# Windowed attention and a gated feed-forward on one core: a first batch ordered by hand, masks added by TensorE, V loaded in place, and y placed behind its a and b

## The chip, the cores and the metric

The kernel runs on one core of a Trainium2 chip. The metric is the device time of one execution in microseconds, as the median of several runs. A profile of one execution was taken by the hardware profiler; its span, the time from the first to the last instruction, was 281.5 us where that run took 283.2 us. The engines are TensorE (matrix products, written to PSUM, a memory of eight banks), VectorE, ScalarE, GpSimd (here used to start the loads) and SyncE (here used to start the stores). Each engine takes its instructions strictly in the order of its own queue, and the engines wait for one another on semaphores.

## The reference

Two parts follow each other. The first is attention over q, k, v of 8 batches, 8 heads, 576 positions and 64 channels. A query sees only keys behind it: in heads 0 to 3 the last 32 positions ("plain"), in heads 4 to 7 the last 32 positions of every fourth ("dilated").

```python
scores = scale * np.matmul(q, k.transpose(0, 1, 3, 2))
rel = pos[:, None] - pos[None, :]
mask_plain = (rel >= 0) & (rel < window)                                  # window = 32
mask_dil = (rel >= 0) & (rel < window * dilation) & (rel % dilation == 0) # dilation = 4
masks = [mask_plain if h < H // 2 else mask_dil for h in range(H)]
attn = softmax(np.where(masks, scores, -1e9))
x = (attn @ v).transpose(0, 2, 1, 3).reshape(B * S, H * D)   # 4608 tokens x 512
a = x @ w1                                                   # 512 -> 1024
b = x @ w2
out = ((a * b) @ w3) @ w_out                                 # 1024 -> 1024 -> 512
```

## The kernel before

**Loads.** All inputs are f32 in HBM and are cast to bf16 by the transfers, which GpSimd starts. `load_qk` fetches q and k of a batch, `load_vp` the values of the plain heads in overlapping blocks of 128 keys, `load_vd` those of the dilated heads into a staging tile `vst`, from which `spread_vd` (L147) copies them to `vd`, where each block of 64 values stands beside a column of ones. The ones make the value product give the softmax's sum as a 65th column. `load_w12`, `load_wo` and `load_w3` fetch the weights. The first loads are, in order: q and k of batch 0's dilated heads, the constants of GpSimd, `vst`, q and k of the plain heads, `vp`, the first halves of w1 and w2, all of batch 1, the second halves of w1 and w2, w_out, and w3 in four pieces.

**Attention.** A batch is four steps: dilated heads, first and second half of the positions (called d0 and d1), then plain heads, first and second half (p0 and p1). u is 1 for the dilated heads and 0 for the plain ones. Before them VectorE transposes q and k, so that channels lie on partitions (`transpose_qk`, L222 and L229). A step has three phases:

- `scores` (L258): for four heads and three blocks of 96 queries, products with the 128 keys of the block, in two halves of 32 channels, so that the four heads use the four quarters of the rows of the array. All go to `ps_a`, four PSUM banks. ScalarE takes exp of all four heads (L269) into `et`, and VectorE multiplies `et` by a mask of ones and zeros (L272). In batch 0 exp and mask work on two heads at a time.
- `values` (L297): 12 products of `et` with the values into the rest of the same banks (in batch 0 into two banks of their own, `ps_e`), then VectorE takes the reciprocal of the sums (L305) and multiplies (L306) into `xo`.
- `to_channels` (L323): six transposes on TensorE into the bank `ps_x`, and a copy into `XT`, the transposed x that lasts for the whole kernel (L338 on ScalarE for the dilated heads, L336 on VectorE for the plain ones).

**Feed-forward.** Tokens go in 9 tiles of 512. `ffn1(t, f)` makes, for one of 8 blocks f of 128 hidden channels, a and then b, of four matmuls of 512 columns each (L425), both into banks `f` of a ring of three. ScalarE copies a to `asb` (L435); VectorE multiplies b by it into `gt` (L436). Since nothing stands between w3 and w_out, the kernel makes their product once: `fuse_t` transposes a block of w3 on TensorE into `ps_x` (L474) and ScalarE copies it to `w3T` (L480); `fuse_m` multiplies it by w_out (L488) and VectorE copies it to `wf_sb` (L495). `ffn2(t, tb)` makes y for 128 tokens with eight matmuls (L458), ScalarE copies it to `osb` (L466, three buffers) and SyncE stores it.

**Order.** The kernel writes every engine's order by hand. Batch 0 runs first, alone. Then comes the first tile's a and b, the fusing, the second tile's a and b, the first tile's y, and from then on the a and b of tile t interleaved with the y of tile t-1: two f, then one block of y. The attention phases of the batches from 1 on are put between the groups of matmuls: `point()` is called before each a, each b and each half of a y or of a fused product, counts the calls and runs as many phases as the table `marks` asks for at that count. `later` appends a phase to the list, `behind` attaches work to the last one. Phases of the steady part come every second point, ahead of an a or of a y. Work attached with `behind`, such as the transposes of the next q and k, follows the values phase on VectorE.

The softmax here doesn't subtract the row's maximum and nothing guards it: scores larger than these inputs give would overflow.

## Time and profile before

| | |
|---|---|
| median of 3 runs | 283.26 us (283.12 to 283.83) |
| span of the profile | 281.5 us |
| TensorE busy | 245.9 us (87%) |
| VectorE busy | 160.1 us (57%) |
| ScalarE busy | 117.8 us (42%) |
| first matmul of a tile (L425) starts | 25.94 us |
| first transposes of w3 (L474) start | 44.41 us |
| a and b of the second tile start | 71.27 us |
| a and b of the third tile start | 105.01 us |
| L425 | 550 matmuls recorded, mean 387 ns |
| L458 | 282 matmuls recorded, mean 379 ns |

The starts are read from TensorE's timeline. A matmul's duration in these lists includes the time that it spends in the pipeline behind its forerunner, so the distance between starts, not the duration, says how fast a stream runs. A releaser in brackets, such as `[3.49 <-DVE kt L222]`, says how long the engine sat idle before the line and which instruction ended the wait. In the names, PE is TensorE, PEld its weight loads, DVE VectorE, ACT ScalarE, POOL GpSimd and SP SyncE.

### The profile page before, as it was taken

The numbers are of one execution on the slowest core, as the hardware profiler recorded it, in microseconds if no ns is written. First come the engines' busy times: TensorE is split into PE (matmuls) and PEld (weight loads), VectorE is DVE, ScalarE is ACT, GpSimd is POOL, SyncE is SP. The second block draws the span as 40 slices with busy tenths as digits, with TensorE's granted clock in tenths as the row PEclk, the third lists the DMA queues.
The fourth block names the chain that finished last, engine by engine and source line by source line (L and its number), as shares of the span: only waits on it lengthen the run. The fifth ranks groups of instructions, "written<-read, shape, count | busy, mean of one in ns | idle before, by whom it ended". The sixth has DMA issues, their size and how long they took to land.

```text
span 281.5 us, 5593 instructions
## 1 busy us (share of the span) xinstructions
PE 245.9 (87%) x2300; PEld 125.7 (45%) x2336; DVE 160.1 (57%) x328; ACT 117.8 (42%) x172; POOL 53.6 (19%) x77
## 2 busy tenths in 40 slices
PE   0355987788958899999999999999999999999994
PEld 0243434454424444545554545545545544444441
DVE  5662268455796776776777777766744632122210
ACT  1552235552435345535433554454345332432331
POOL 8943512450070060024006000000000000000000
PEclk9999999999989999999999999999999999999998
DMA  7999999999179289589747912110111121111233
GB/s 104 155 204 194 194 210 211 208 186 178 9 131 148 30 157 225 90 131 156 109 88 126 172 42 60 55 41 37 40 37 40 37 75 40 48 64 40 57 82 123
DMA packets 50745, 30.50 MB, mean 108 GB/s; under 512 B 37920, under 2 KB 40992, under 8 KB 50720
## 3 DMA queue, kind: packets, MB, share of 16 engines
q0 software_dynamic: 45088, 20.71, 58.7%
q1 hardware_dynamic: 5632, 9.44, 10.8%
q8 instruction: 18, 0.29, 0.4%
q14 instruction: 7, 0.06, 0.1%
HBM read 41.41 MB, written 9.44 MB: 181 GB/s over the span
## 4 chain that ended last, share of the span: by engine, by line
PE 75%; DMA 9%; DVE 6%; POOL 3%; ACT 3%; issue 2%; POOLq 0%; ACTq 0%; DVEq 0%
PE f L425 39%; PE f L458 22%; DMA qn<-in_q_dram 5%; DMA w_sb<-in_moe_w_dram 4%; PE ps_a L258 4%; PE f L488 4%; PE ps_a L297 3%; PE ps_x L323 3%; DVE xo L306 2%; ACT w3T L480 1%; PE ps_x L474 1%; POOL vst L136 1%; DVE gt L436 1%; DVE qt L229 1%; ACT et L269 1%
## 5 line engine op out<-in xcount | busy, mean ns | idle before, releaser
L425 PE MATMUL f<-XT,w_sb 128*128 128x512 bf16 x550 | 136.5, 387 | 3.4 <-issue 0.9
L436 DVE TENSOR_TENSOR gt<-f,asb 128x512 bf16<-128x512 f32 x72 | 49.6, 689 | 63.8 <-PE f L425 61.5
L425 PEld LDWEIGHTS <-w_sb 128*128 128x128 bf16 x576 | 53.6, 99 | 62.6 <-issue 5.8
L458 PE MATMUL f<-wf_sb,gt 128*128 128x512 bf16 x282 | 67.2, 379 | 0.4 <-issue 0.2
L435 ACT CAST asb<-f 128x512 bf16<-128x512 f32 x72 | 42.3, 587 | 53.4 <-PE f L425 52.0
L466 ACT COPY osb<-f 128x512 f32<-128x512 f32 x36 | 21.1, 586 | 70.2 <-PE f L458 68.2
L269 ACT ACTIVATE et<-ps_a 128x1152 bf16<-128x1152 f32 (+1 forms) x36 | 36.5, 1026 | 18.3 <-PE ps_a L258 18.3
L458 PEld LDWEIGHTS <-gt 128*128 128x128 bf16 x288 | 26.5, 98 | 28.5
L258 PE MATMUL ps_a<-qt,kt 32*128 32x96 bf16 x768 | 15.1, 211 | 18.5 <-DVE kt L229 7.9
L306 DVE TENSOR_TENSOR xo<-ps_a,rcp 96x768 bf16<-96x768 f32 x28 | 26.7, 953 | 1.0
L258 PEld LDWEIGHTS <-kt 32*128 32x128 bf16 x768 | 10.9, 97 | 30.5 <-issue 16.9
L136 POOL DMA_DIRECT2D vst<-in_v_dram x32 | 21.2, 669 | 14.1 <-DMA w3n<-in_moe_w_dram 4.4
L229 DVE STREAM_TRANSPOSE qt<-qn 128x160 uint32<-128x160 uint32 (+1 forms) x64 | 19.6, 420 | 2.3 <-DMA qn<-in_q_dram 2.3
L272 DVE TENSOR_TENSOR et<-et,mask_pl 128x1152 bf16<-128x1152 bf16 (+1 forms) x18 | 12.4, 692 | 14.3 <-ACT et L269 14.2
L297 PEld LDWEIGHTS <-et 128*128 128x128 bf16 x384 | 16.9, 102 | 7.4 <-issue 1.4
L323 PE MATMUL ps_x<-ident,xo 96*128 96x96 bf16 x192 | 14.4, 214 | 6.6 <-DVE xo L306 4.0
L323 PEld LDWEIGHTS <-xo 96*128 96x128 bf16 x192 | 12.0, 102 | 14.3 <-DVE xo L306 5.2
L272 DVE TENSOR_TENSOR et<-et,mask_di 128x1152 bf16<-128x1152 bf16 (+1 forms) x18 | 12.3, 687 | 9.8 <-ACT et L269 9.7
L112 POOL DMA_DIRECT2D qn<-in_q_dram x9 | 6.2, 690 | 57.8 <-DVE qt L229 54.6
L488 PE MATMUL f<-wo_sb,w3T 128*128 128x512 bf16 x60 | 15.1, 379 | 0.4 <-issue 0.3
L338 ACT COPY XT<-ps_x 128x576 bf16<-128x576 bf16 x18 | 11.5, 640 | 9.2 <-PE ps_x L323 9.1
L480 ACT COPY w3T<-ps_x 128x1024 bf16<-128x1024 bf16 x8 | 8.1, 1012 | 8.4 <-PE ps_x L474 8.4
(45 smaller groups left out, 111.3 us busy)
## 6 DMA issues: line engine op xcount, KB each, us to landing
qn<-in_q_dram POOLq DMA_DIRECT2D x7, 576.0 KB, 6.1
kn<-in_k_dram POOLq DMA_DIRECT2D x7, 576.0 KB, 7.8
vp<-in_v_dram POOLq DMA_DIRECT2D x7, 384.0 KB, 10.5
w_sb<-in_moe_w_dram POOLq DMA_DIRECT2D x4, 512.0 KB, 11.5
w3n<-in_moe_w_dram POOLq DMA_DIRECT2D x4, 512.0 KB, 18.7
out_dram<-osb SPq DMA_DIRECT2D x8, 256.0 KB, 2.3
out_dram<-osb SPq DMA_DIRECT2D x8, 224.0 KB, 2.4
out_dram<-osb SPq DMA_DIRECT2D x8, 192.0 KB, 2.2
```

The costliest lines, as they stand in the source:

```text
L136: nc.gpsimd.dma_start(out=vsts[b % 2][p0 : p0 + n, m, :, :], in_=bass.AP(tensor=x.tensor, offset=x.offset + (4 * i0 + 2 * second) * D, ap= ...
L258: nc.tensor.matmul(out=ps_a[:, h, c0 : c0 + 96], lhsT=kt[prt, 96 * m : 96 * m + P, c], rhs=rhs, start=(c == 0), stop=(c == 1),)
L269: nc.scalar.activation(out=ev, in_=ps_a[:, h : h + n, 0:HALF], func=ACT.Exp, scale=scale)
L272: nc.vector.tensor_tensor(out=ev, in0=ev, in1=mk.unsqueeze(1).to_broadcast([P, n, HALF]), op=AL.mult)
L297: nc.tensor.matmul(out=ov[:, j // ns, j % ns, :], lhsT=self.et[:, c0 : c0 + P], rhs=rhs, start=True, stop=True,)
L306: nc.vector.tensor_tensor(out=xo[0:96].rearrange("p h j d -> p (h j) d").rearrange("p (n s) d -> p n s d", n=nb), in0=ov[0:96, :, :, 0:D], ...
L323: nc.tensor.transpose(out=xo, in_=self.xo[0:96, hp, 2 * m : 2 * m + 2, :], identity=ident[0:96, 0:96],)
L425: nc.tensor.matmul(out=ps, lhsT=w_sb[:, c, f * P : (f + 1) * P], rhs=XT[:, c, t0 + lo : t0 + hi], start=(c == 0), stop=(c == DCH - 1),)
L435: nc.scalar.copy(out=a_sb[:, 0 : hi - lo], in_=ps)
L436: nc.vector.tensor_tensor(out=gts[t][:, f, lo:hi], in0=pss[1], in1=a_sb[:, 0 : hi - lo], op=AL.mult)
L458: nc.tensor.matmul(out=y, lhsT=gts[t][:, f, tb * P : (tb + 1) * P], rhs=wf_sb[:, f, :], start=(f == 0), stop=(f == KFF - 1),)
L488: nc.tensor.matmul(out=ps, lhsT=w3T[ft][:, g, :], rhs=wo_sb[:, g, :], start=(g == 0), stop=(g == KFF - 1),)
```

## The change

The change rewrites the beginning and one thing in the steady part.

- **The first batch is written out by hand** (`first_batch`), in pairs of heads. `scores_of_pair` first lets TensorE put the mask into PSUM, as the product of the identity with a tile of 0 and -30000 (`neg_pl`, `neg_di`), one matmul of 288 columns for each head, and adds the scores to it. So exp gives zeros outside the window, and the multiplication on VectorE goes. The masks of ones and zeros that the later batches use are made at the end of the batch (`const_masks`).
- **PSUM has a layout of its own in that stage**: two pairs of banks for scores (`ps_s`), a ring of three banks for values (`ps_o`), and `ps_x`. Afterwards the seven become the ring `f` of three and `ps_a` of four.
- **V of the dilated heads is loaded straight into place.** A row of `vd` now holds a one, 64 values, 64 values and a one, so that each half position has a one beside it. The staging tile and `spread_vd` go. In `normalize` the sums are the first column for d0 and the last for the others.
- **Loads have another order**: q and k of the plain heads come ahead of V; w1 and w2 come whole, in three pieces each, then w_out in halves, then w3 mixed with batch 1. The plain values of the first three batches are loaded in two transfers. Prefetching of a batch sits one phase later.
- **Batch 1 has a table of points** (`second_batch`): its phases run at points 19 to 38, that is, in the fusing and in the first y.
- **The fused product**: transposes of w3 go to banks of the ring instead of `ps_x`, half of the copies to `w3T` (three buffers now) go to VectorE, and a product is made in two halves with a point ahead of each.
- **y stands right behind its own a and b**: a tile is 8 f, then 4 blocks of y. The first y comes before the second tile's a and b. `osb` has six buffers. The marks are moved, and the phases of the steady part now fall ahead of a b or of the second half of a y.

The core of the diff:

```diff
-    ps_a = psum.tile([P, 4, TB], F32, name="ps_a")
     ps_x = psum.tile([P, 2 * TB], BF16, name="ps_x")
-    ps_e = ps_early.tile([P, 2, TB], F32, name="ps_e")
+    ps_s = [ps_early.tile([P, 2, TB], F32, name=f"ps_s{i}") for i in range(2)]
...
-                out=vsts[b % 2][p0 : p0 + n, m, :, :],
+                out=vds[b % 2][p0 : p0 + n, 4 * m : 4 * m + 4, 16 : 16 + 2 * D],
...
+        def scores_of_pair(self, hp):
+            ps = ps_s[hp]
+            neg = (neg_di if self.u else neg_pl[:, self.hf]).rearrange("p m x -> p (m x)")
+            for g in range(2):
+                nc.tensor.matmul(
+                    out=ps[:, g, 0:HALF], lhsT=ident, rhs=neg, start=True, stop=False
+                )
+            self.score_matmuls((2 * hp, 2 * hp + 1), lambda h: ps[:, h % 2], False)
+            nc.scalar.activation(
+                out=self.probs(2 * hp, 2), in_=ps[:, :, 0:HALF], func=ACT.Exp, scale=scale
+            )
...
+    def first_batch():
+        d0, d1, p0, p1 = steps[0:4]
+        transpose_qk(0, 1, 0)
+        transpose_qk(0, 1, 1)
+        d0.scores_of_pair(0)
+        d0.scores_of_pair(1)
+        transpose_qk(0, 0, 0)
+        transpose_qk(0, 0, 1)
+        d1.scores_of_pair(0)
+        d1.scores_of_pair(1)
+        p0.scores_of_pair(0)
+        p0.scores_of_pair(1)
+        d0.values_of_pair(0)
+        d0.values_of_pair(1)
+        p1.scores_of_pair(0)
+        d1.values_of_pair(0)
+        p1.scores_of_pair(1)
+        d1.values_of_pair(1)
+        d0.to_channels()
+        p0.values_of_pair(0)
+        p0.values_of_pair(1)
+        d1.to_channels()
+        p1.values_of_pair(0)
+        p1.values_of_pair(1)
+        p0.to_channels()
+        p1.to_channels()
+        const_masks()
+        prefetch(2)
...
+            (19, transpose_qk, 1, 1, 0),
+            (20, transpose_qk, 1, 1, 1),
+            (22, d0.scores),
+            (24, d1.scores),
+            (26, d0.values),
+            (28, transpose_qk, 1, 0, 0),
+            (28, d0.to_channels),
+            (28, d1.values),
+            (29, transpose_qk, 1, 0, 1),
+            (30, p0.scores),
+            (30, d1.to_channels),
+            (32, p1.scores),
+            (34, p0.values),
+            (36, p0.to_channels),
+            (36, p1.values),
+            (36, prefetch, 3),
+            (38, p1.to_channels),
...
-        xv = ps_x.rearrange("p (g x) -> p g x", g=KFF)
+        xv = bank().bitcast(BF16).rearrange("p (g x) -> p g x", g=KFF)
...
-        w3T[ft] = wk_pool.tile([P, KFF, P], BF16, tag="w3T", bufs=2, name="w3T")
-        nc.scalar.copy(out=w3T[ft], in_=xv)
+        w3T[ft] = wk_pool.tile([P, KFF, P], BF16, tag="w3T", bufs=3, name="w3T")
+        (nc.vector.tensor_copy if ft % 2 else nc.scalar.copy)(out=w3T[ft], in_=xv)
...
-    load_qk(0, split=True)
+    load_qk(0, 1)
+    const_pool()
+    load_qk(0, 0)
+    load_vd(0)
     load_vp(0)
-    load_w12(0, 512)
-    load_qk(1)
-    load_vd(1)
-    load_vp(1)
-    load_w12(512, 1024)
-    load_wo()
-    for g in range(4):
-        load_w3(g)
+    load_w12(0, 256)
+    load_w12(256, 512)
+    load_w12(512, 1024)
+    load_wo(0)
+    load_wo(1)
+    load_w3(0)
+    load_w3(1)
+    load_qk(1, 1)
+    load_w3(2)
+    load_vd(1)
+    load_w3(3)
+    load_qk(1, 0)
+    load_vp(1)
...
-    for t in range(2, NT):
-        for i in range(4):
-            ffn1(t, 2 * i, point)
-            ffn1(t, 2 * i + 1, point)
-            ffn2(t - 1, i, point)
-    for tb in range(4):
-        ffn2(NT - 1, tb, point)
+    for t in range(1, NT):
+        for f in range(KFF):
+            ffn1(t, f, point)
+        for tb in range(4):
+            ffn2(t, tb, point)
```

## The prediction

> **What bounds the kernel now.** I read the busy times first (TensorE 87% of the span), then the chain of waits, then busy time by stage, with the stage borders taken from TensorE's timeline. The columns are stretch, length, and busy us of TensorE, its weight loads, VectorE, ScalarE and GpSimd.
>
> ```profile
> 7.93:25.94 18.01, 8.05 (x169) 6.76 (x170) 10.41 (x22) 8.59 (x13) 10.55 (x14) 1.00 1.36 191
> 25.94:44.41 18.47, 17.08 (x110) 7.15 (x112) 8.96 (x21) 6.74 (x10) 6.45 (x9) 1.00 1.43 199
> 44.41:71.50 27.09, 21.62 (x247) 13.09 (x251) 14.28 (x24) 11.64 (x12) 8.23 (x10) 1.00 1.43 189
> 71.50:105.46 33.96, 28.49 (x345) 14.55 (x350) 27.30 (x59) 14.88 (x21) 10.50 (x14) 0.95 0.72 96
> 105.46:130.60 25.14, 24.93 (x261) 12.72 (x265) 18.18 (x36) 12.05 (x19) 5.91 (x8) 1.00 0.98 150
> ```
>
> The last line is one tile beside one batch, 25.14 us with TensorE never idle. In the chain it is a repeated pattern of 16 `L425` and 8 `L458` matmuls in 6.285 us. Without attention, from 229 us on, the same 24 take 5.18 us: 0.2158 us a matmul, and 1.10 us of TensorE for one attention step (scores, values, transposes). So the whole program needs, after the first batch, 928 matmuls (9 tiles of 96, 64 for W3·W_out) x 0.2158 = 200.3, 64 weight transposes x 0.058 = 3.7, and 28 steps x 1.1 = 30.8: 234.8 us. Tiles start at 25.94, the last matmul ends at 278.1, and 3.4 us of eviction and store follow. 278.1 - 25.94 - 234.8 = 17.4 us are lost, all before 105.5: some 4 in the second line, 6 in the third and 8 in the fourth. What can be won is there and in the first 25.94 us.
>
> ```profile
> 5.52 1.20 DVE L229 STREAM_TRANSPOSE qt<-qn 128x160 uint32<-128x160 uint32 x4 [1.15 <-DMA qn<-in_q_dram]
> ...
> 11.49 1.22 DVE L229 STREAM_TRANSPOSE qt<-qn 128x160 uint32<-128x160 uint32 x4 [1.16 <-DMA qn<-in_q_dram]
> ...
> 14.39 1.24 DVE L222 STREAM_TRANSPOSE kt<-kn 128x576 uint32<-128x576 uint32 x1
> ...
> 15.69 0.67 PE L258 MATMUL ps_a<-qt,kt 32*128 32x96 bf16 x24 [3.49 <-DVE kt L222]
> ...
> 24.55 0.66 PE L323 MATMUL ps_x<-ident,xo 96*128 96x96 bf16 x6 [1.31 <-DVE xo L306]
> ...
> 25.25 0.64 ACT L338 COPY XT<-ps_x 128x576 bf16<-128x576 bf16 x1 [1.99 <-PE ps_x L323]
> 25.94 0.58 PE L425 MATMUL f<-XT,w_sb 128*128 128x512 bf16 x1 [0.73 <-ACT XT L338]
> ```
>
> In the first batch the plain heads' q is transposed only at 11.49 and their k at 14.39, though VectorE could have done so at 8.1. Every step's scores, mask, values, normalising and transposing follow one another. The last XT copy ends at 25.89 and tiles start.
>
> ```profile
> 19.14 1.43 POOL L129 DMA_DIRECT2D vp<-in_v_dram  x1 [1.83 <-DMA w_sb<-in_moe_w_dram]
> ...
> 52.40 0.70 POOL L112 DMA_DIRECT2D qn<-in_q_dram  x1 [1.27 <-DMA w3n<-in_moe_w_dram]
> ```
>
> GpSimd waits in the brackets are landings: its eight DMA semaphores go round, so an issue waits for the one eight before it. The first w1 half landed at 19.1 and all of w3 at 52.4. In destination bytes the loads up to there are 2,396 KB and 8,892 KB: 195 KB/us.
>
> ```profile
> 123.50 0.44 PE L258 MATMUL ps_a<-qt,kt 32*128 32x96 bf16 x24
> ...
> 124.08 1.14 ACT L269 ACTIVATE et<-ps_a 128x1152 bf16<-128x1152 f32 x1
> ...
> 125.11 0.59 ACT L435 CAST asb<-f 128x512 bf16<-128x512 f32 x1
> 125.25 0.76 DVE L272 TENSOR_TENSOR et<-et,mask_di 128x1152 bf16<-128x1152 bf16 x1 [0.69 <-ACT et L269]
> ...
> 125.93 0.68 DVE L436 TENSOR_TENSOR gt<-f,asb 128x512 bf16<-128x512 f32 x1
> ...
> 127.59 0.53 PE L297 MATMUL ps_a<-vd,et 128*128 128x65 bf16 x12
> ...
> 128.47 0.22 DVE L305 RECIPROCAL rcp<-ps_a 96x12 f32<-96x12 f32 x1
> 128.73 0.95 DVE L306 TENSOR_TENSOR xo<-ps_a,rcp 96x768 bf16<-96x768 f32 x1
> 129.60 1.24 DVE L229 STREAM_TRANSPOSE qt<-qn 128x160 uint32<-128x160 uint32 x4
> ...
> 129.78 0.44 PE L258 MATMUL ps_a<-qt,kt 32*128 32x96 bf16 x24
> ```
>
> This is the steady step. Scores at 123.50 give `et` at 125.22 and the mask at 125.25 to 125.93. VectorE takes work in order, so `gt`, whose b was filled by then, starts only at 125.93. Values at 127.59 occupy VectorE from 128.47 to 129.60 and a transpose of 1.1 us follows; the next scores at 129.78 come just after `xo`.
>
> **What the Trainium skill says.** "TensorE: Matmul & The Clock Gate", What's actually happening: the array runs at 1.2 GHz until it was busy for about 3.4 us, then at 2.4. The trace agrees: the first ten `L425` matmuls, from 26.7, are 0.427 us apart, later ones 0.216. The same page, Back-to-back issue gap: N/1.2 ns cold, N/2.4 + 2.5 warm; that prices a 288-column mask matmul at 0.24 or 0.12 us, which no run here shows yet. "TensorEngine Tiling (Array Packing)", Key Properties: row tiles work in parallel, and changing the mode drains the array. By the price above 24 scores of 96 columns would take 1.9 us cold one after another; they take 0.67, so four heads do run together, and with two heads I expect half the rate. "VectorE: DVE Perf Modes", The perf-mode tier table: copies from PSUM reach at most 2x. The 128x576 XT copy takes 0.45 us on VectorE, so 1024 bf16 elements take about 0.7 us (estimate), against 1.01 on ScalarE.
>
> **The change part by part.**
>
> *First batch.* Removed: 8 mask multiplications (0.45 us each), the 1.47 us spread of V on ScalarE, and the late q and k loads (now issued at about 4.2 instead of 6.83). Added: 16 mask matmuls, 3.8 us cold, and scores at half the rate, 8 pairs x 0.48 cold. Chain: k transposed at 8.0, first exp at 8.65 as now. q and k of the plain heads land at 8.5 to 10 and are transposed by 11.5. Eight exps of 0.65 us on two score buffers come every 0.75 to 1.0 us, the last two after `et` 0 is free at about 13.8: all by 16. Eight normalisings are 0.2 + 0.5 us (half of 0.95), so 6 us of VectorE, from 13.6, when vd lands; vp lands at about 16.5, as now. They end at 20.2 to 21.3. Then a transpose (0.45) and XT (0.64) give the tile start: 21.3 warm, 23.2 cold. I take 22.0, with the array warm from the dense score work, so the first tile does not pay its ten cold matmuls (2.1 us).
>
> *Load order.* w1 and w2 come before batch 1, in pieces. At 200 KB/us from vp on: first pieces at 19.2, last at 26.8, wanted at 29; w_out 31.8; w3 from 34.3, wanted at 36; batch 1's dilated q, k 38.2 and 39.7, plain 48.3 and 49.7. All are hidden by the tile's own matmuls.
>
> *First tile.* No attention is inside it now: 22.0 + 13.8 + 0.2 = 36.0 (now 44.41).
>
> *Fusing W3·W_out with batch 1, then the first y.* Half the w3T copies go to VectorE and w3 transposes get banks from the ring of three instead of ps_x, which takes away the waits of both kinds of transpose on one bank. I followed the built order against the durations above. VectorE then carries 8 wf_sb copies (0.62 pitch), 4 w3T (0.7), 4 transposes (1.1), 4 masks (0.7), 4 normalisings (1.2), 2 XT copies (0.45): 20.7 us. Its queue is solid from about 48 to 56, and the plain k transpose comes at 54.7 to 55.95. The plain scores, ordered ahead of the second half of the seventh product, stand in TensorE's queue from 53.45 to 56.05 and hold everything behind them: 2.6 us. In all 3.2 us lost. Needed: 17.5 + 6.9 + 4.4 = 28.8, so the second tile starts at 68.0. The kernel now has done the same work at about 78 (71.3 plus the 6.9 us of the first y).
>
> *Second tile.* The transposes of batch 2 run on VectorE beside the end of the first y. Then `gt` stands behind a transpose or a mask that waits for exp; three banks give b only some 2.0 us until its bank is wanted (a, transposes and b of the next). By the built order about 1.0 us is lost at the second b and 0.9 at three of the scores behind `xo`, smaller bits elsewhere: 4.7 of 30.5. Third tile from 98.5.
>
> *Tiles 3 to 7, y right behind.* Nothing is saved on TensorE, which has no gaps there. The b's come every 1.73 us for 13.8 us, and the attention pieces now fall between a and b instead of ahead of a. After scores, exp waits for a's copy on ScalarE and `gt` for the mask, and ends 3.4 us after the scores' start; its bank is wanted after b, a, transposes and b, at 3.2: 0.2 to 0.25 us late. After values, `gt` waits for normalising and a transpose: again about 0.25. Three or four such places are 0.8 us a tile, 4.0 in five tiles. y's last matmul of the first group needs the last `gt` 0.9 us after b; seven matmuls (1.5 us) cover that. Six osb buffers, V in place (0.55 us less VectorE a batch), prefetch one phase later: hidden, or in the above.
>
> *Sum.* 22.0 + 234.8 + 3.4 + lost 0.2 + 3.2 + 4.7 + 4.0 = 272.3 span. The profiled span is 1.8 below the time (281.5 against 283.26): **274.0 us**.
>
> **The rivals.**
> A: grouping costs nothing and the first batch is warm early. Tile start 21.3, lost 0.2 + 3.2 + 3.0 (second tile): 265.9 span, 267.7 us. For it: ScalarE and VectorE have average room in a tile (12 and 18 of 25 us). Against it: order on VectorE, not its sum, makes the waits.
> B: the middle stages lose what they lose now, 6.3 and 7.8 us in place of 3.2 and 4.7: 6.2 more, 280.2 us. For it: VectorE is 80% busy from 71.5 to 105.5, and nothing of that load but the spread goes. Against it: the weight transposes' waits on ps_x go.
> C: the ring of three banks becomes the bound. The only stretch of now that has a's and b's without y's between, 71.3 to 95.4, holds 13.8 us of matmuls and 4.1 of attention, and lost 6.2. Half of that for each of five tiles, since attention is thinner there, is 15.5 instead of 4.0: 285.5 us, slower than before. Against it: per tile VectorE has 6 us of room.
>
> **How the numbers follow.** The forecast has 0.50, A 0.25, B 0.17, C 0.08. A, B and the forecast are faster; C is slower, and a time within 0.3% is left 0.01 of that: 0.92 faster, 0.01 same, 0.07 slower. The range takes in A's end less a little and B's plus a little, 267 to 281. The ends of the unknown costs (mask matmuls cold or warm: 1.9 us at the start and up to 2.1 in the first tile; bank waits 0 to 1.5 us a tile) lie within it.
>
> **What would show it.** Right: the first tile's matmuls start at 21 to 23.5, at 0.216 apart; the second tile's at 66 to 71; a wait of TensorE for the plain k transpose in the fusing stage; idle TensorE of 0.3 to 1.5 us in each of tiles 3 to 7, ended by `gt`. Wrong: a first matmul after 24.5; waits for w_sb or w3n above 1 us; 27 us or more for a tile beside attention; gapless tiles of 25.1 would make A right.

## The result and the profile after

The changed kernel takes 271.99 us (median of 4 runs, 269.81 to 273.12), beside 283.19 us for the kernel before on the same chip: a ratio of 0.9605, 95% interval 0.9531 to 0.9679. The profiled run has a span of 270.2 us (281.5 before). Forecast were 274.0 us and a span of 272.3, so the total was near. Some terms of the sum were not, and the total is near in part by luck: errors in both directions cancelled, as worked out below. All ratios leave out executions in a slower state, of which the experiments had one (with the old order of the loads).

| start of | before | forecast | after |
|---|---|---|---|
| first tile | 25.94 | 22.0 | 23.50 |
| fusing | 44.41 | 36.0 | 39.09 |
| second tile, same work done | 78.2 | 68.0 | 70.54 |
| third tile, same work done | 111.9 | 98.5 | 100.05 |
| end of the span | 281.5 | 272.3 | 270.2 |

(For before, 6.9 us, the first y, are added to 71.27 and to 105.01, since the changed kernel has then done one y more.) The lead over before grows from 2.4 us to 5.3, 7.7 and 11.9, and stays (11.3 at the end): the gain is made ahead of 100 us. Busy time by stage, cut at those starts (stretch, length, busy us of TensorE, its weight loads, VectorE, ScalarE and GpSimd with instructions in brackets, granted clock, DMA share, GB/s):

```profile
7.80:23.50 15.70, 14.11 (x183) 9.26 (x183) 8.70 (x24) 7.75 (x12) 10.46 (x14) 1.00 1.53 184
23.50:39.09 15.59, 15.59 (x64) 6.70 (x64) 4.84 (x7) 4.68 (x8) 4.63 (x7) 1.00 1.17 210
39.09:70.54 31.45, 28.95 (x329) 16.23 (x328) 22.60 (x48) 11.49 (x13) 14.24 (x18) 1.00 1.54 196
70.54:100.05 29.51, 26.99 (x325) 13.71 (x324) 22.27 (x46) 14.76 (x20) 6.91 (x9) 1.00 0.91 137
100.05:125.20 25.15, 25.15 (x265) 12.72 (x264) 18.10 (x36) 12.23 (x18) 5.50 (x7) 1.00 0.86 121
```

In the first line TensorE is busy 14.11 of 15.70 us, where before it was busy for 8.05 of 18.01: most of the first batch is now bound by TensorE. In the second it never idles, but the same 64 matmuls take 15.59 us instead of the 13.8 that they need. In the third 2.5 us are idle and in the fourth as many. The last is a tile beside attention with y right behind, as the next ones are: TensorE is busy the whole of it, and it takes what such a tile took before (25.15, the next 25.14).

The first batch in the timeline (start, duration, engine, line, operation):

```profile
8.39 0.66 PE L280 MATMUL ps_s<-neg_di,ident 128*128 128x288 bf16 x2
8.49 0.65 ACT L284 ACTIVATE et<-ps_s 128x576 bf16<-128x576 f32 x1 [6.47 <-PE ps_s L264]
...
8.98 0.66 PE L264 MATMUL ps_s<-qt,kt 32*128 32x96 bf16 x12
...
9.57 0.66 PE L280 MATMUL ps_s<-neg_di,ident 128*128 128x288 bf16 x2
9.68 0.65 ACT L284 ACTIVATE et<-ps_s 128x576 bf16<-128x576 f32 x1 [0.54 <-PE ps_s L264]
...
10.87 0.65 ACT L284 ACTIVATE et<-ps_s 128x576 bf16<-128x576 f32 x1 [0.54 <-PE ps_s L264]
...
22.13 0.64 PE L355 MATMUL ps_x<-ident,xo 96*128 96x96 bf16 x6 [0.73 <-ACT XT L370]
...
22.81 0.64 ACT L370 COPY XT<-ps_x 128x576 bf16<-128x576 bf16 x1 [0.73 <-PE ps_x L355]
23.50 6.69 PE L502 MATMUL f<-XT,w_sb 128*128 128x512 bf16 x22 [0.73 <-ACT XT L370]
```

One pair of heads takes 1.19 us of TensorE: from 8.39 to 8.98 two mask matmuls, then 12 scores until 9.57. The exps come at the same distance (8.49, 9.68, 10.87), each after idling for TensorE. At the end, from 18.7 us on, the one bank `ps_x` sets the pace: transposes, 0.64 us of copy, the next transposes, 1.37 us a round. And with all this the array is still slow at 23.50. Its weight loads in the first tile show it:

```profile
25.59 0.15 PEld L502 LDWEIGHTS <-w_sb 128*128 128x128 bf16 x1 [0.27 <-issue]
26.01 0.15 PEld L502 LDWEIGHTS <-w_sb 128*128 128x128 bf16 x1 [0.28 <-issue]
```

0.43 us lie between them, not 0.216, and so on until about 27.2.

The steady step, to be laid beside the one of before:

```profile
101.01 0.45 PE L264 MATMUL ps_a<-qt,kt 32*128 32x96 bf16 x24
...
101.65 1.14 ACT L294 ACTIVATE et<-ps_a 128x1152 bf16<-128x1152 f32 x1
102.82 0.76 DVE L295 TENSOR_TENSOR et<-et,mask_pl 128x1152 bf16<-128x1152 bf16 x1 [1.05 <-ACT et L294]
...
103.39 1.89 PE L502 MATMUL f<-XT,w_sb 128*128 128x512 bf16 x8
103.50 0.68 DVE L513 TENSOR_TENSOR gt<-f,asb 128x512 bf16<-128x512 f32 x1
...
105.11 0.53 PE L306 MATMUL ps_a<-vd,et 128*128 128x65 bf16 x12
...
107.68 1.90 PE L502 MATMUL f<-XT,w_sb 128*128 128x512 bf16 x8
107.89 0.67 DVE L513 TENSOR_TENSOR gt<-f,asb 128x512 bf16<-128x512 f32 x1
```

`gt` still stands behind the mask (102.82, 0.76 us) on VectorE, as before, and is as late again behind normalising and transposes (107.89). But no TensorE line has an idle bracket: nothing of TensorE waits for it.

The loads and the wait in the fusing stage:

```profile
36.66 0.70 POOL L164 DMA_DIRECT2D w3n<-in_moe_w_dram  x1 [1.72 <-DMA w3n<-in_moe_w_dram]
...
47.90 0.57 POOL L138 DMA_DIRECT2D vd<-in_v_dram  x1 [0.47 <-DMA qn<-in_q_dram]
49.56 0.75 POOL L138 DMA_DIRECT2D vd<-in_v_dram  x1 [1.09 <-PE ps_a L264]
```

```profile
56.17 0.68 DVE L573 CAST wf_sb<-f 128x512 bf16<-128x512 f32 x1
56.77 0.68 DVE L557 COPY w3T<-f 128x1024 bf16<-128x1024 bf16 x1
57.37 1.24 DVE L229 STREAM_TRANSPOSE kt<-kn 128x576 uint32<-128x576 uint32 x1
...
58.67 0.44 PE L264 MATMUL ps_a<-qt,kt 32*128 32x96 bf16 x24 [1.84 <-DVE kt L229]
```

w3's last piece is issued at 36.66; the plain q of batch 1 had landed at 47.9 (the GpSimd line waited for it), k by 49.56, when the issue eight behind its own went out. So both are there well ahead of VectorE's transpose at 57.37: k waits in VectorE's queue, behind the two copies and the normalising, and TensorE waits 1.84 us for it.

### The profile page after: what moved, and what is told of

Read it like the earlier page. It is cut to its first block, busy times and chain, and to the rows that moved or that the text cites. A ratio compares the mean times of both kernels' runs of the same rounds, so it can differ in the third digit from the quotient of the medians.

```text
span 270.2 us, 5648 instructions
## 1 busy us (share of the span) xinstructions
PE 252.3 (93%) x2352; PEld 127.6 (47%) x2352; DVE 158.4 (59%) x329; ACT 113.7 (42%) x167; POOL 57.8 (21%) x84
## 4 chain that ended last, share of the span: by engine, by line
PE 87%; DVE 7%; ACT 2%; DMA 2%; issue 1%; POOL 0%; POOLq 0%; DVEq 0%
PE f L502 45%; PE f L535 23%; PE ps_a L264 4%; PE ps_x L355 4%; PE f L565 3%; PE ps_a L306 3%; DMA kn<-in_k_dram 2%; PE ps_s L264 2%; DVE xo L314 2%; PE ps_s L280 1%; ACT XT L370 1%; ACT et L294 1%; DVE qt L236 1%; DVE kt L229 1%; DVE et L295 1%; DVE gt L513 1%
## 5 line engine op out<-in xcount | busy, mean ns | idle before, releaser
L513 DVE TENSOR_TENSOR gt<-f,asb 128x512 bf16<-128x512 f32 x72 | 49.4, 687 | 48.3 <-PE f L502 44.0
L535 PE MATMUL f<-wf_sb,gt 128*128 128x512 bf16 x288 | 68.0, 379 | 0.0
L294 ACT ACTIVATE et<-ps_a 128x1152 bf16<-128x1152 f32 x28 | 31.7, 1134 | 14.0 <-PE ps_a L264 14.0
L138 POOL DMA_DIRECT2D vd<-in_v_dram x32 | 21.3, 672 | 41.9 <-PE ps_a L306 32.4
L264 PEld LDWEIGHTS <-kt 32*128 32x128 bf16 x768 | 12.2, 97 | 22.5 <-issue 16.9
L295 DVE TENSOR_TENSOR et<-et,mask_pl 128x1152 bf16<-128x1152 bf16 x14 | 10.6, 758 | 12.8 <-ACT et L294 12.8
L295 DVE TENSOR_TENSOR et<-et,mask_di 128x1152 bf16<-128x1152 bf16 x14 | 10.6, 756 | 10.4 <-ACT et L294 10.4
L565 PE MATMUL f<-wo_sb,w3T 128*128 128x512 bf16 x64 | 16.0, 380 | 0.7 <-ACT w3T L557 0.7
L264 PE MATMUL ps_a<-qt,kt 32*128 32x96 bf16 x672 | 12.4, 202 | 4.1 <-DVE xo L314 2.3
L313 DVE RECIPROCAL rcp<-ps_a 96x12 f32<-96x12 f32 x28 | 6.3, 224 | 15.4 <-PE ps_a L306 15.4
L114 POOL DMA_DIRECT2D qn<-in_q_dram x10 | 6.6, 662 | 30.5 <-DVE qt L236 26.1
```

The lines of the kernel that those rows point to most:

```text
L264: nc.tensor.matmul(out=bank_of(h)[:, c0 : c0 + 96], lhsT=kt[prt, 96 * m : 96 * m + P, c], rhs=rhs, start=(start and c == 0), stop=(c == 1 ...
L294: nc.scalar.activation(out=ev, in_=ps_a[:, :, 0:HALF], func=ACT.Exp, scale=scale)
L295: nc.vector.tensor_tensor(out=ev, in0=ev, in1=mk.unsqueeze(1).to_broadcast([P, 4, HALF]), op=AL.mult)
L513: nc.vector.tensor_tensor(out=gts[t][:, f, lo:hi], in0=pss[1], in1=a_sb[:, 0 : hi - lo], op=AL.mult)
L535: nc.tensor.matmul(out=y, lhsT=gts[t][:, f, tb * P : (tb + 1) * P], rhs=wf_sb[:, f, :], start=(f == 0), stop=(f == KFF - 1),)
L565: nc.tensor.matmul(out=wf_ps[ft], lhsT=w3T[ft][:, g, :], rhs=wo_sb[:, g, :], start=(g == 0), stop=(g == KFF - 1),)
```

## The experiments

Each kernel is the changed kernel with the edit shown, except two that are the kernel before with parts of the change. Times are medians with the ratio to the kernel before measured beside them. The changed kernel's own ratio is 0.9605. In some of the expectations batches are counted from 1: the "batch 2" of the fusing stage there is batch 1 of this text.

**V through the staging tile again.** The loads of the dilated V go to `vst`, and a copy brings them to `vd`.

```diff
-                out=vds[b % 2][p0 : p0 + n, 4 * m : 4 * m + 4, 16 : 16 + 2 * D],
+                out=vsts[b % 2][p0 : p0 + n, 4 * m : 4 * m + 4, :],
...
+    def spread_vd(b):
+        copy = nc.vector.tensor_copy if b else nc.scalar.copy
+        copy(out=vds[b % 2][:, :, 16 : 16 + 2 * D], in_=vsts[b % 2])
```

> The changed kernel with V of the dilated heads loaded into a staging tile again and copied into place, by ScalarE in the first batch and by VectorE after it (0.55 us each). In tiles 3 to 7 gt ends 0.07 us before its bank is wanted after scores, and hardly earlier after values. Theory 1, the tiles run at the edge of the three banks: the copy, which stands behind a values phase and its transpose, makes one gt a tile late by about 0.5 us: tiles of 25.5 to 25.7 us instead of 25.15, plus 0 to 1 us in the fusing and the second tile: 274 to 276 us. Rival, there is room: tiles stay at 25.15, 272 to 272.7 us.

271.95 us, ratio 0.9608 (0.9557 to 0.9660): no different. In the steady part the copy costs VectorE 0.56 us and TensorE nothing:

```profile
103.71 1.89 PE L511 MATMUL f<-XT,w_sb 128*128 128x512 bf16 x8
...
105.90 1.90 PE L511 MATMUL f<-XT,w_sb 128*128 128x512 bf16 x8
106.11 0.56 DVE L150 COPY vd<-vst 128x1536 bf16<-128x1536 bf16 x1
...
106.57 0.69 DVE L522 TENSOR_TENSOR gt<-f,asb 128x512 bf16<-128x512 f32 x1
```

This tells more than the time. The `gt` of 106.57 to 107.26 reads the b that ended at about 104.6. Two groups later, in the middle of the burst that starts at 105.90 (x8 is a b and the next a), that a starts at about 106.76 without idling, while the old b is still being read. So this a doesn't go into that bank. The programs as built agree. Of the TensorE instructions of the changed kernel, here are the first matmul of the third b, the fourth a and b and the fifth a of the third tile, with the engine that each waits for:

```
1926 L502 Matmult f_1549<-XT_79,w2_sb_76 128x512 [waits DVE_49]
1934 L502 Matmult f_1555<-XT_79,w1_sb_75 128x512 [waits DVE_49]
1990 L502 Matmult f_1588<-XT_79,w2_sb_76 128x512 [waits Activation_49]
1998 L502 Matmult f_1594<-XT_79,w1_sb_75 128x512 [waits Activation_49]
```

If the three banks went strictly round, as the forecast took them to, the fifth a (`f_1594`) would wait for VectorE's `gt` of the third b (`f_1549`). It waits for ScalarE instead. In the built program the third b lies in bank 3, the fourth and the fifth a both in bank 1, which ScalarE's copy of the fourth a has freed, and bank 3 comes back only with the fifth b. This looser order is what hides the copy here: a strict ring would have waited 0.5 us, from 106.76 to 107.26.

In the changed kernel itself a strict ring would have cost hardly anything, because the times of the forecast were too long as well. In the steady step shown above, `gt` ends at 104.18, which is 3.17 us after the scores' start and not 3.4, and the a that a strict ring would put into its bank starts at about 104.25 (four matmuls of 0.216 behind 103.39). Behind normalising, `gt` ends at 108.56 and that a starts at about 108.54. So the forecast's bank waits in tiles 3 to 7 rested on two things that did not hold: banks strictly in turn, and times some 0.2 us too long in each place.

The profile of this run shows one thing more. The first batch gives TensorE the same matmuls as in the changed kernel, but here the array has its full speed ahead of the first tile:

```profile
21.17 0.42 PE L360 MATMUL ps_x<-ident,xo 96*128 96x96 bf16 x6
...
23.45 13.97 PE L511 MATMUL f<-XT,w_sb 128*128 128x512 bf16 x64 [0.73 <-ACT XT L375]
```

Six transposes take 0.42 us from 21.17 on (0.64 in the changed kernel still at 22.13), and the first tile takes 13.81 us instead of 15.59. The trace's record of the granted clock begins at 21.07, the changed kernel's at 27.13. So the time at which the array gets its full speed is not fixed by this first batch, and a difference of 2 us in the first tile of a single profile says nothing of an edit.

**Masks by VectorE in the first batch.** Pairs, layout and order stay; the masks of ones and zeros are made early and multiplied as before; the plain q is transposed a place earlier.

```diff
-            for g in range(2):
-                nc.tensor.matmul(
-                    out=ps[:, g, 0:HALF], lhsT=ident, rhs=neg, start=True, stop=False
-                )
-            self.score_matmuls((2 * hp, 2 * hp + 1), lambda h: ps[:, h % 2], False)
+            self.score_matmuls((2 * hp, 2 * hp + 1), lambda h: ps[:, h % 2], True)
...
+            nc.vector.tensor_tensor(
+                out=ev, in0=ev, in1=mk.unsqueeze(1).to_broadcast([P, 2, HALF]), op=AL.mult
+            )
```

> The changed kernel with the first batch's masks multiplied in on VectorE after exp, as in the kernel before, and no mask matmuls; the plain q transpose is put ahead of the first mask in VectorE's order. Theory 1, TensorE bounds the first batch up to the first transposes at 18.0: 16 mask matmuls of 0.3 us leave its queue, and the first tile starts at 21 to 22 instead of 23.5: 270 to 271 us. Rival, VectorE, with eight masks of 0.45 us more, becomes the bound of the batch: first tile at 23.5 to 25, 272 to 273.5 us. The tiles after the fusing are untouched either way: 25.15 us each.

270.74 us, 0.9572 (0.9530 to 0.9614). The time alone is not told apart from the changed kernel's, the profile is: the first tile starts at 22.09 instead of 23.50 (23.45 to 23.68 in the six profiles that have the mask matmuls and no fillers), takes 15.74 (15.59), the fusing stage 31.45 (31.45) and a steady tile 25.14. So adding the masks on TensorE costs 1.4 us in this stage rather than saving anything, since TensorE is the limit of most of it. What the earlier transpose of q adds to this was not tried by itself.

**The array warmed ahead.** Eighteen matmuls of 128x512 on zeros stand before the first batch, where TensorE waits for q and k.

```diff
+    for _ in range(18):
+        nc.tensor.matmul(
+            out=ps_s[1][:, 0, :], lhsT=warm[:, 0:P], rhs=warm, start=True, stop=True
+        )
     first_batch()
```

> The changed kernel with 18 matmuls of 128 rows x 512 columns on a tile of zeros put ahead of the first batch, into a bank that the first mask overwrites; the output is the same. Theory 1, the first batch is bound by a cold array (mask and score matmuls of a pair 0.59 us each): the array is at full clock after some 4 us, the pairs come every 0.7 us instead of 1.19, the first tile starts at 20.5 to 21.5 instead of 23.5 and needs 13.9 us instead of 15.6: about 267.5 us. Rival, the work of the first batch does not count as busy for the array's clock, so it falls back within a few us: the first tile starts at 23 to 23.5, again with some ten matmuls at 0.43 us: within 1 us of the changed kernel's 272.

268.96 us, 0.9499 (0.9448 to 0.9550). A pair now takes about 0.8 us and the first tile starts at 20.03, 3.5 us earlier. But it takes 16.68 us. The stretches around its start (columns as above):

```profile
18.00:19.00 1.00, 0.35 (x5) 0.30 (x6) 0.96 (x4) 0.53 (x1) 0.43 (x2) 1.00 1.45 197
19.00:20.00 1.00, 0.30 (x3) 0.17 (x4) 0.33 (x2) 0.64 (x1) 0.36 (x2) 0.52 1.34 202
...
22.00:24.00 2.00, 2.00 (x6) 0.76 (x5) 0.28 (x1) 0.56 (x1) 0.15 (x1) 0.50 1.25 208
...
26.00:28.00 2.00, 2.00 (x11) 0.90 (x10) 0.69 (x1) 0.58 (x1) 0.70 (x1) 1.00 1.25 208
```

From 18 to 20 us TensorE is busy for a third of the time; the granted clock falls to a half and comes back only after six microseconds of dense work. Warming pays, and the gaps at the batch's end take a part of it back.

**All copies to w3T on ScalarE**, and the plain q of batch 1 transposed five points earlier.

```diff
-        (nc.vector.tensor_copy if ft % 2 else nc.scalar.copy)(out=w3T[ft], in_=xv)
+        nc.scalar.copy(out=w3T[ft], in_=xv)
...
+            (23, transpose_qk, 1, 0, 0),
             (24, d1.scores),
             (26, d0.values),
-            (28, transpose_qk, 1, 0, 0),
```

> The changed kernel with all eight w3T copies on ScalarE and the plain q transpose of batch 1 at point 23 instead of 28. Theory, the wait of 1.84 us for the plain k transpose comes from VectorE's queue, solid from 50.4 to 58.6: 3 copies of 0.6 us and 1.1 us of transpose leave it ahead of that transpose, the wait goes and the second tile starts 1.5 to 1.9 us earlier, near 68.8: 270.2 us. Rival, ScalarE with 1.01 us a copy and exp in the same queue now holds the products: a wait for w3T appears and the second tile starts at 70 to 71: 272 us.

271.45 us, 0.9571 (0.9508 to 0.9635). The wait for the plain k falls from 1.84 to 0.90 us and the stage from 31.45 to 30.51. Half of it was VectorE's load. In the profiled span (270.4) it is lost, because in this profile the first tile took 16.7 us instead of 15.6: where the array gets its full clock is not the same in every execution.

**y interleaved again.**

```diff
-    for t in range(1, NT):
-        for f in range(KFF):
-            ffn1(t, f, point)
-        for tb in range(4):
-            ffn2(t, tb, point)
+    for f in range(KFF):
+        ffn1(1, f, point)
+    for t in range(2, NT):
+        for i in range(4):
+            ffn1(t, 2 * i, point)
+            ffn1(t, 2 * i + 1, point)
+            ffn2(t - 1, i, point)
...
-        marks.append((15 + 24 * t, done_at[4 * t + 3]))
+        marks.append((6 + 24 * t, done_at[4 * t + 3]))
```

> Only the order of the middle tiles is put back: a and b of the second tile alone, then from the third tile on two a, b groups and one y of the tile before in turn. First batch, fusing stage, loads and layouts are the changed kernel's. Theory (right behind each block the y give batch 3 room: 23 points to spread its phases over instead of 14): up to the end of the fusing stage nothing changes (second tile starts at about 70.5 us plus what the first tile's start differs), the second tile's a and b together lose more than the 2.5 us they lose now, 2 to 4 us more in all, and the time is 274 to 276 us; the later tiles keep 25.15 us. Rival (the order of y is free as long as the array has work; the gain is all in the first batch and in the fusing stage): 272 us within 0.5, and the second tile's losses stay about 2.5 us.

277.8 us, 0.9800 (0.9740 to 0.9860): 5.8 us worse, more than expected, and the steady rhythm is the same (two f and one y in 6.29 us, four of them 25.15). All but 0.7 us of it is lost in the second tile, where the third batch now has 14 points instead of 23; the order and the fewer points were not tried apart. Timeline of TensorE there, and its clock:

```profile
79.27 0.44 PE L264 MATMUL ps_a<-qt,kt 32*128 32x96 bf16 x24 [2.25 <-DVE xo L314]
79.64 1.89 PE L502 MATMUL f<-XT,w_sb 128*128 128x512 bf16 x4
```

```profile
79.00:82.00 3.00, 2.73 (x35) 1.50 (x35) 2.65 (x7) 1.56 (x2) 0.00 (x0) 0.60 1.08 203
82.00:85.00 3.00, 2.66 (x21) 1.14 (x19) 1.43 (x3) 0.94 (x3) 1.02 (x2) 0.83 0.71 133
```

Scores wait 2.25 us for `xo` (0.75 in the changed kernel), and then the granted clock drops: four matmuls take 1.89 us in the list where they took 1.04. So the wait costs itself and then nearly 2 us more of half speed (0.60 and 0.83 over two stretches of 3 us are 3.4 us at a half). The profile of the kernel before has the same: TensorE idles for 2.23 us for `xo` until 81.76, and the granted clock is 0.50 from 82.0 to 85.4 us. The changed kernel has no such stretch in its second tile, which is a part of its gain there.

**The old order of the loads.**

```diff
-    load_w12(0, 256)
-    load_w12(256, 512)
-    load_w12(512, 1024)
...
+    load_w12(0, 512)
+    load_qk(1)
+    load_vd(1)
+    load_vp(1)
+    load_w12(512, 1024)
+    load_wo(0)
+    load_wo(1)
+    for g in range(4):
+        load_w3(g)
```

> Only the order of the weight loads is put back in the changed kernel: w1 and w2's first halves, then batch 1's q, k and v, then the second halves, wo and w3, instead of w1, w2, wo and w3 ahead of most of batch 1. Theory (the first tile, which now starts 2.4 us earlier, would outrun the second halves): TensorE waits in the first tile for w1 and w2's second halves, by 2 to 5 us, and the time is 274 to 277 us; the wait of 1.84 us for the plain k of batch 1 in the fusing stage shrinks or goes. Rival (there is slack in the loads, their order is hidden): 272 us within 0.5, without a TensorE wait for w_sb.

276.88 us (three runs, 276.27 to 279.83), 0.9809 (0.9726 to 0.9893): 5 to 6 us worse. TensorE's waits from 22 to 76 us (total, times, longest):

```profile
PE f L502 <- DMA w_sb<-in_moe_w_dram: 2.7, 2, 1.5
PE ps_a L264 <- DVE kt L229: 1.8, 1, 1.8
PE f L551 <- DMA w3n<-in_moe_w_dram: 1.3, 1, 1.3
```

The two DMA lines are 4.0 us. Fusing starts at 44.12 instead of 39.09, and the wait for the plain k (L229) is what it was: it is not a wait for k to land.

**w3's transposes through ps_x again.**

```diff
-        xv = bank().bitcast(BF16).rearrange("p (g x) -> p g x", g=KFF)
+        xv = ps_x.rearrange("p (g x) -> p g x", g=KFF)
...
-        w3T[ft] = wk_pool.tile([P, KFF, P], BF16, tag="w3T", bufs=3, name="w3T")
-        (nc.vector.tensor_copy if ft % 2 else nc.scalar.copy)(out=w3T[ft], in_=xv)
+        w3T[ft] = wk_pool.tile([P, KFF, P], BF16, tag="w3T", bufs=2, name="w3T")
+        nc.scalar.copy(out=w3T[ft], in_=xv)
```

> Only the fusing stage's transposes of w3 go back to the one bank ps_x, all copied by ScalarE into two buffers, instead of the ring of three banks and two engines. Batch 2's own transposes share ps_x then. Theory (the ring of banks lets transposes and copies run beside the matmuls): each of the eight copies, about 1 us, is waited for in part, 2 to 4 us in all; the fusing stage takes 33.5 to 35.5 us instead of 31.45 and the time is 274 to 276 us. Rival (the transposes were hidden by one matmul group ahead in either way): fusing stage 31 to 32 us, time 272 within 0.5.

272.17 us, 0.9615 (0.9566 to 0.9665), and the stage takes 31.39 us (31.45). Waits on `ps_x` appear (1.1 and 0.3 us), and the wait for k shrinks (0.9 instead of 1.84), since VectorE makes four copies less. The rival is right on the time: the ring and the copies on VectorE together are worth nothing here. The ring by itself may be worth something: with it, and with all copies on ScalarE and the q transpose earlier, the stage took 30.51 us.

**Loads, grouped y and late batch 1 on the kernel before.** Its first batch, PSUM layout, masks and staging are left as they were. Batch 1's phases are spread evenly over points 19 to 40.

```diff
-    marks = [
-        (0, n0), (9, n0), (30, done_at[7]), (32, done_at[7]), (54, done_at[11]),
-    ]
-    for t in range(3, 8):
-        marks.append((54 + 24 * (t - 2), done_at[4 * t + 3]))
+    marks = [(0, n0), (19, n0), (40, done_at[7])]
+    for t in range(2, 8):
+        marks.append((15 + 24 * t, done_at[4 * t + 3]))
```

(The loads and the loop over tiles are the changed kernel's, as in the diffs above read backwards; `osb` has six buffers.)

> The kernel before, with its own first batch, PSUM layout, VectorE masks and V staging, but with the changed kernel's order of weight loads (batch 1's loads for each of q, k, V behind w1, w2, wo, w3), its grouped y and its points for batch 2 and later. Theory (loads and grouping carry nearly all; the first batch by hand is worth only its 2.4 us at the start of the first tile): first tile starts at about 26, first tile without a wait for w_sb 13.8 to 15, fusing at 40 to 41, span 272 to 273.5 and time 274 to 275.5 us. Rival (the three depend on each other, and the loads in the new order come too late or the old first batch needs more): 277 us or more.

279.51 us, 0.9863 (0.9816 to 0.9909): the expectation failed, by 4 to 5 us. The first tile starts at 26.93 and takes 15.9, 1 us beyond what was expected each, but the stage from fusing to the second tile takes 35.24 us. TensorE's waits in that stretch:

```profile
PE ps_a L257 <- DVE xo L305: 2.5, 2, 1.9
PE ps_x L322 <- ACT w3T L479: 1.2, 1, 1.2
PE ps_x L473 <- ACT w3T L479: 1.1, 1, 1.1
PE ps_x L322 <- DVE xo L305: 0.9, 2, 0.4
```

**The same, with batch 1 at the points of the change.**

```diff
+    for at, f, *args in (
+        (19, transpose_qk, 1, 1, 0),
+        (20, transpose_qk, 1, 1, 1),
+        (20, spread_vd, 1),
+        (22, d0.scores),
...
+        (36, prefetch, 3),
+        (38, p1.to_channels),
+    ):
+        later(f, *args)
+        when.append(at)
...
-        while state[1] < want:
+        while state[1] < want and (state[1] >= n1 or state[0] >= when[state[1]]):
```

> As the run on the kernel before with the new loads and the grouped y, but batch 2's phases stand at the changed kernel's hand-written points (19 to 38) instead of being spread evenly over points 19 to 40; ps_x for w3's transposes, V staging, VectorE masks by pairs in the first batch and the old first batch stay. Theory (the 3.8 us that the fusing stage was longer in that run come from where batch 2's phases stand, not from the one bank ps_x, which cost 0.2 us in the changed kernel): the fusing stage takes 31.5 to 33 us, time 275.5 to 277.5. Rival (ps_x shared by w3's transposes and batch 2's output costs it): stage 34.5 to 35.5, time 279 to 280.

274.79 us, 0.9686 (0.9636 to 0.9736), 4.7 us less, and the stage takes 31.39 us. The waits for `xo` are gone; those on the shared `ps_x` stay in part:

```profile
PE ps_x L497 <- ACT w3T L503: 1.1, 1, 1.1
PE ps_a L257 <- DVE kt L221: 0.9, 1, 0.9
PE ps_x L322 <- ACT w3T L503: 0.3, 1, 0.3
```

So where batch 1's phases stand is a part of the change by itself, and a large one. The forecast had not named it.

**Towards a better version.** The fillers were put into the gaps too, together with the copies on ScalarE and the early q:

```diff
         p0.to_channels()
+        warm_up(3)
         p1.to_channels()
+        warm_up(4)
```

> The changed kernel with 18 matmuls of 128x512 on zeros ahead of the first batch, three more behind the third and four behind the fourth block of output transposes of the first batch (where TensorE waits 0.73 us and about 1.0 us for the copy to XT), and all eight copies of w3T on ScalarE with the plain q transposed five points earlier. Theory (the array warms with dense wide matmuls alone and falls back in the gaps at 17.7 to 20 us): the first tile starts at 20.0 to 20.4 us and takes 13.8 us, all of it at 0.216 us a matmul; fusing starts at 33.9 to 34.3, the stage takes 30.5, and the time is 264 to 266 us. Rival (the fall back does not come from these gaps, but from the sparse stage as a whole): the first tile starts cold and takes 15.5 to 17 us, time 267 to 268.5 us.

269.69 us, 0.9526 (0.9469 to 0.9583). The theory on the gaps holds: the first tile's 64 matmuls start at 21.03 and run through in 13.97 us. But the early q now stands in VectorE's queue before it has landed (49.3 us): VectorE waits 3.7 us, TensorE 2.1 for `wf_sb` behind it, and the clock drops again. The stage takes 34.2 us. With the fillers alone:

> The changed kernel with the 18 matmuls on zeros ahead of the first batch, and the three and four in the gaps at the end of it; the copies of w3T and the q transpose as in the changed kernel. Theory (the run before lost 3.7 us of VectorE, and with it 2.1 us of TensorE, at the plain q moved ahead of its landing): first tile starts at 20.0 to 21.0 and takes 13.8 to 14.6, fusing at 34 to 35.6, the stage keeps 31.5 to 32.5, as the plain q and k of batch 1 land no earlier than about 48 and 49.6, so that the wait for kt grows to 2.5 to 4 us; time 267 to 268.5 us. Rival (the landing of batch 1 holds the second tile where it was, all the gain ahead of fusing is given back): 270 to 272 us.

270.34 us, 0.9530 (0.9485 to 0.9576), in the rival's range, though not for its reason. The first tile takes 13.81 us, 22.54 to 36.35; it starts late because the granted clock was a half within the first batch, from 13.0 to 19.8 us. The fusing stage takes 33.0. The theory had the wait for k grow; it is the same 1.84 us, with a consequence that the changed kernel did not have:

```profile
55.93 0.44 PE L266 MATMUL ps_a<-qt,kt 32*128 32x96 bf16 x24 [1.84 <-DVE kt L231]
...
56.57 2.87 PE L575 MATMUL f<-wo_sb,w3T 128*128 128x512 bf16 x8
```

```profile
57.00:58.00 1.00, 1.00 (x5) 0.40 (x4) 0.41 (x1) 1.00 (x2) 0.00 (x0) 0.67 2.08 164
58.00:59.00 1.00, 1.00 (x4) 0.25 (x2) 0.95 (x2) 0.08 (x1) 0.81 (x2) 0.50 2.36 161
59.00:60.00 1.00, 1.00 (x27) 0.49 (x26) 0.00 (x0) 0.00 (x0) 1.00 (x2) 0.50 2.25 180
```

Eight matmuls take 2.87 us in the list (1.89 in the changed kernel's profile, after the same wait): the granted clock falls to a half for about three microseconds. Then batch 1's plain half was moved two points later:

```diff
+            (28, d0.to_channels),
+            (28, d1.values),
+            (30, d1.to_channels),
+            (30, transpose_qk, 1, 0, 0),
+            (32, transpose_qk, 1, 0, 1),
+            (33, p0.scores),
+            (35, p1.scores),
+            (36, p0.values),
+            (38, p0.to_channels),
+            (38, p1.values),
```

> As the run with the fillers in the gaps, and the plain half of batch 2 moved two points later in the fusing stage. Theory (with TensorE 3 to 4 us earlier, batch 2's plain half stands too early for the landing of q and k; two points are about 3 us): the wait for kt is 0 to 1 us, the stage takes 30.5 to 31, the second tile's losses grow by 0 to 1 us, time 265 to 266.5 us. Rival (the crowding only moves on into y of the first tile and the second tile's start, where p1's output of batch 2 is needed): the second tile loses 2 us or more beyond, time 267 to 269 us, as without the shift.

268.45 us (267.29 to 270.03), 0.9482 (0.9422 to 0.9542), the lowest of all, though not told apart from the array warmed ahead alone (268.96). First tile 13.81, stage 31.04, second tile 29.54. The wait for k is 0.3 us, but the first tile began at 21.91 this time, after 1.7 us of waiting for `vp` to land. So the expected 265 to 266.5 us were missed; the time is in the rival's range, but the second tile lost nothing more (29.51 in the changed kernel).

## Why the forecast was right in sum, and where its terms were not

*Start of the first tile, 22.0 forecast, 23.50 measured.* The bounds of 21.3 warm and 23.2 cold were right in kind: warmed by fillers, the start was 20.03 (21.03 to 22.54 in the three later runs with fillers, which waited for k or `vp` or fell back in between). The choice between them was wrong. It took TensorE's price for masks (1.9 us more if cold) as something beside other work; it is the path, 1.4 us of it. A pair of heads was also priced too low, 0.48 us for its masks and 0.48 for its scores, where it took 1.19. One reading of the prediction doesn't hold: in the kernel before VectorE could not have transposed the plain q at 8.1, since its line at 11.49 waits for q to land. It is the earlier load that brings this transpose to 8.24.

*First tile, 13.8 forecast, 15.59 measured.* The term "the array warm from the dense score work" failed in this profile. The Trainium skill, "TensorE: Matmul & The Clock Gate", Part 1 on the clock gate, has the array warm after about 3.4 us of busy time. Here 14.1 busy of 15.7 us did not do it. With the staging tile the same matmuls did, at 21.07 us, so whether this term comes true is in part luck. These matmuls are narrow (96, 65 and 288 columns) and the scores use 32 rows each; which of these counts was not tried.

*Load order hidden.* Right. No TensorE wait for w_sb or w3n, and the old order in the new kernel costs 5 to 6 us. Batch 1's plain q was forecast to land at 48.3 and landed at 47.9.

*Fusing and first y, 32.0 forecast, 31.45 measured.* The size was right, and so was the wait for the plain k (2.6 forecast, 1.84 measured; VectorE's transpose came at 57.37, 18.3 us after the stage's start, forecast 18.7). The reason given for the gain was not: the ring of banks and the two engines for the copies bring nothing together (0.2 us), while the points at which batch 1 stands are worth 4.7 us against an even spread over the same stretch.

*Second tile, 30.5 forecast, 29.51 measured.* The three waits behind `xo` came as forecast (0.9 each; 0.75 measured). The 1.0 us at the second b did not come. TensorE was idle for 2.5 us, where 4.7 were forecast, but its work was 27.0 us and not 25.8 (30.5 less 4.7): two errors that partly cancel.

*Tiles 3 to 7, 4.0 us lost forecast, none measured.* This is the step that failed most: `gt` "ends 3.4 us after the scores' start; its bank is wanted after b, a, transposes and b, at 3.2". Both times were wrong. `gt` ends after 3.17 us, which alone brings the wait to nothing. And the waits were worked out for banks taken strictly in turn: as built, an a takes the bank that ScalarE has just freed, and `gt` has a microsecond more. By the prediction's own sign, gapless tiles of 25.1 us, rival A's "grouping costs nothing" is right for these tiles; rival C, the ring of three banks as the bound, was wrong for the same reasons as the forecast, only more so.

Start and first tile were 3.1 us too low in the forecast, the stages behind them 1.5 too high, and all from the third tile on 3.7 (4.0 for the bank waits less 0.3 elsewhere); the sum is 2.1 too high. That it is no further off is luck: the errors have opposite signs.

What the gain consists of, in steps that were each run: loads, grouping and a later batch 1 on the kernel before 3.8 us; its points 4.7; the rest, that is the first batch by hand, V in place, w3T and the smaller changes of the loads, 2.8 (differences of medians, each uncertain by a microsecond or so). The single parts depend on one another: undone alone, the loads cost 5 to 6 us and the grouping (with the third batch's points) 5.8, together about as much as the whole change brings. Not tried were the order of q and k ahead of V by itself and the prefetch one phase later.

## What to carry to other kernels

Where a hand-written order meets a start-up stage, place each phase by when its inputs are there, not evenly: the same work at other points was worth 4.7 us here, the new first batch and all the rest 2.8. Before moving work to TensorE because it looks idle, ask what limits the stage afterwards, and count narrow matmuls at the slow clock. A term that depends on when the array reaches full speed needs more than one profile. And don't work out waits for a ring of buffers by counting round: look in the built program which instruction each waits for.

## What the runs showed of the hardware that was not expected

- Dense but narrow matmuls do not reliably bring the array to full speed. It came at 21.07 us, ahead of the first wide matmul, in one profile, and at 26.78 to 29.45, 3 to 6 us into the wide ones, in the five others with the same first batch. In the changed kernel TensorE was busy for 14.11 of 15.70 us, and then matmuls were 0.43 us apart for another 3.7 us. The granted-clock column reads 1.00 in that stretch; only the distance between matmuls tells. Eighteen wide ones on zeros brought it at 5.4 us.
- A gap of TensorE of about two microseconds can halve its clock for about three more: after 2.25 us (interleaved y), 2.23 (the kernel before) and 2.11 (early q) it did; after 1.84 at the same place it did in one profile and not in six others. In the traces every stretch at one clock that ends before the program does is a whole multiple of 3.41 us long. The Trainium skill, "TensorE: Matmul & The Clock Gate", Part 1 on the clock gate, speaks of an idle window of about 3.4 us, and of windows that run free of the program; the measured gaps are shorter than such a window, and its length and the two outcomes of the same gap fit the second statement. What decides between the outcomes is not shown. So an unlucky wait costs twice. Together with the first tile's 13.81 to 16.71 us in profiles with the same first batch and no wait for weights, this may be a source of the 3 us between executions of one kernel.
- Copying V into place once more per batch, 0.56 us of VectorE, was not to be seen in the time at all (271.95 and 271.99 us).
